# A causal mask on the matrix engine, and head operands that leave PSUM once

## The chip, the core and the metric

The kernel runs on one core of a Trainium2 chip. The core has five engines with an instruction queue each: TensorE (PE in the profile, its weight loads PEld), VectorE (DVE), ScalarE (ACT), GpSimd (POOL) and SyncE (SP), which here only issues DMAs. POOL issues DMAs too. An engine works through its own queue in order and waits at an instruction until all that it needs has been done elsewhere. Matmuls write to PSUM, from which DVE and ACT read; POOL works on SBUF only. The metric is the device time of one execution in microseconds (us); lower is better.

## The reference

Two operators stand one behind the other. The first is attention with chunk selection, on q, k and v of 4 batches, 8 heads, 768 positions and 64 dimensions:

```python
k_chunks = k.reshape(B, H, nc, chunk, D)            # 24 chunks of 32 keys
k_min, k_max = k_chunks.min(3), k_chunks.max(3)
ub = sum(maximum(q * k_min, q * k_max), over D)     # a bound for each query and chunk
ub = where(query's chunk >= chunk, ub, -1e9)
sel = the 6 chunks with the largest ub
scores = where(sel & (query >= key), q @ k.T / 8, -1e9)
out = softmax(scores) @ v
```

Its output, 3072 tokens of 512, is the input of a mixture of experts: a dense two-layer network with relu for every token, and one of eight experts of the same form, picked by a gate, whose result is scaled by the gate's probability and added.

## The kernel before

**Tiling.** Heads are worked in pairs: a pair p (16 of them, four to a batch) has two heads g = 0 and 1 with 64 dimensions each, which together fill 128 partitions. Its 768 positions are six tiles of 128.

**Operands of the scores.** Scores are computed transposed, keys on the partitions, by one matmul for each key tile over the query tiles from there on. Its two operands for head g are `kT[p % 3][g]` and `rT[p % 3][g]`, each 128 partitions x 768 columns of f16, three sets in turn. Head 0 has its keys in rows 0 to 63 of `kT`, and in rows 64 to 95 a constant `exf`, which says with 30000 which chunk a key is in. Head 1 has the constant in rows 0 to 31 and its keys in rows 64 to 127. Opposite them `rT` holds the negated queries and, in the rows of the constant, flags: 1 where a chunk is *not* among the query's six. A score of an unselected key so has 30000 added, and since the exponential is taken with a scale of -0.125 (L555), it becomes zero.

**Preparing a pair** takes six steps, which are written out ahead of the pair's own scores:

- `cast_qk`, `cast_v` (L464 to L476): POOL turns q, k and v from f32 to f16.
- `prep_k` (L478): PE transposes the keys into a PSUM tile `pk`, ACT copies them in order of position to an SBUF tile `kp`, DVE reduces that to the largest and smallest of each chunk (`ks`, L495) and masks these by head (`kb`, L498).
- `prep_q` (L505): PE transposes the queries into `pq`; ACT takes relu of it into `qp` (L513), DVE negates it into the first head's operand, all 128 partitions (L514), and the second head's half into the second's (L515).
- `prep_kt` (L500): DVE copies the halves of `kp` into the two `kT` (L502, L503).
- `prep_ub` (L517): PE computes the bounds from `qp`, the negated queries and `kb`, on top of a causal bias; DVE finds the sixth largest of each row with `max` (L531) and sets the flags (L533).
- `prep_s` (L535): PE transposes the flags and DVE copies them into the flag rows of both `rT` (L541, L542), over the negated queries that the bounds have read.

**The loop over a pair** has eleven units (L210 to L219), each of up to four blocks of 128 keys x 128 queries. In the program's order, unit i of all pairs computes the scores two units ahead, then does one step of preparation (`prep_s` of the next pair at unit 2, `prep_k` of the pair but one at unit 4, `prep_q` at 5, `prep_kt` at 7, `prep_ub` at 9), then fills from the dense network of the batch before, then the product with v (`av`) and the norm of the unit before. Three units of a pair hold the blocks on the diagonal, four each (units 0, 5 and 6). Their exponentials go through POOL, which sets to zero what lies above the diagonal (`affine_select`, L557) before the product with v reads them.

**Order on POOL and SP.** The casts are held behind the last instruction in `latest["pool"]`, which is L557 before the change: `cast_v` of the pair but one at unit 0, `cast_qk` of the third pair ahead at unit 7. Behind them POOL issues weight DMAs (from pair 1 on) and, in batches 1 to 3, scatters the tokens of the batch before to a table in DRAM (L370). SP issues the loads of q, k and v, two buffers each, once a cast has freed one, and stores the dense results.

**PSUM.** In attention three buffers are shared by `pk`, `pq`, `ub`, `ps` and all tiles of the fills, three hold scores and two the products with v.

Behind attention comes the expert stage, with the last batch's dense work beside the expert blocks; its lines (L672 on) are not touched.

Of the kernel before, what the change touches and what calls it, by code (L numbers as in the profile page):

```python
# [10 lines left out]
HF = mybir.dt.float16  # L11
AF = mybir.ActivationFunctionType
ALU = mybir.AluOpType
# [4 lines left out]
def kernel(  # L18
# [12 lines left out]
    nc = tc.nc  # L31
    B, H, S, D = q.shape
# [32 lines left out]
    NJ = 2  # L65
# [10 lines left out]
    acst = att.enter_context(tc.tile_pool(name="acst", bufs=1))  # L76
# [24 lines left out]
    NB = 3  # L101
# [29 lines left out]
                                fill=-60000.0, base=j, pattern=[[128, NT], [0, 2], [-32, NC]], channel_multiplier=2)  # L131
    for i in range(NB):
        nc.vector.memset(kT[i][0][64:128], 0.0)
        nc.vector.memset(kT[i][1][0:64], 0.0)
        nc.vector.memset(v16[i][:, :, :, D : D + 1], 1.0)

    def members():
# [2 lines left out]
        nc.gpsimd.affine_select(out=exf[0:32], in_=exf[0:32], compare_op=ALU.is_ge, fill=0.0,  # L140
                                base=31, pattern=[[-1, S]], channel_multiplier=32)

    def expand(i):
        nc.scalar.copy(kT[i][0][64:96, :], exf[0:32])
        nc.scalar.copy(kT[i][1][0:32, :], exf[0:32])


    iom8 = const.tile([128, NT, E], FP)
# [308 lines left out]
    with (  # L457
# [20 lines left out]
        def prep_k(p):  # L478
            s = st[p]
            pk = pprep.tile([128, S], HF, name="pk", tag="pp")  # L480
            for t in range(NT):
                nc.tensor.transpose(pk[:, t * 128 : (t + 1) * 128], s["k16"][:, t].rearrange("p g d -> p (g d)"), ident)  # L482
            s["kp"] = kp = ahead.tile([128, S], HF, name="kp")
            nc.scalar.copy(kp.rearrange("d (T p j) -> d T p j", p=128, j=NJ),  # L484
                           pk.rearrange("d (T j p) -> d T p j", p=128, j=NJ))
            ks = ahead.tile([128, 2, NC], HF, name="ks")
            if p == 0:

                pc = pk.rearrange("d (T j c w) -> d T c j w", j=NJ, c=8, w=16)
                for i, op in enumerate((ALU.max, ALU.min)):  # L490
                    nc.vector.tensor_reduce(out=ks[:, i].rearrange("d (T c) -> d T c", c=8), in_=pc, op=op,
                                            axis=mybir.AxisListType.XY)
            else:
                for i, op in enumerate((ALU.max, ALU.min)):
                    nc.vector.tensor_reduce(out=ks[:, i], in_=kp.rearrange("d (c w) -> d c w", w=32), op=op,  # L495
                                            axis=mybir.AxisListType.X)
            s["kb"] = kb = ahead.tile([128, 2, 2, NC], HF, name="kb")
            nc.vector.tensor_tensor(kb, ks.unsqueeze(2).to_broadcast([128, 2, 2, NC]), hmask, ALU.mult)  # L498

        def prep_kt(p):  # L500
            kp = st[p]["kp"]
            nc.vector.tensor_copy(kT[p % NB][0][0:64], kp[0:64])  # L502
            nc.vector.tensor_copy(kT[p % NB][1][64:128], kp[64:128])  # L503

        def prep_q(p):  # L505
            s = st[p]
            pq = pprep.tile([128, S], HF, name="pq", tag="pp")
            pqv = pq.rearrange("d (T h j p) -> d T h j p", h=2, j=NJ, p=64)
            for t in range(NT):
                nc.tensor.transpose(pqv[:, t // NJ, :, t % NJ], s["q16"][:, t].rearrange("p g d -> p (g d)"), ident)  # L510
            s["qp"] = qp = ahead.tile([128, S], HF, name="qp")
            r0, r1 = rT[p % NB]
            nc.scalar.activation(qp, pq, AF.Relu)  # L513
            nc.vector.tensor_single_scalar(r0, pq, -1.0, ALU.mult)  # L514
            nc.vector.tensor_single_scalar(r1[64:128], pq[64:128], -1.0, ALU.mult)  # L515

        def prep_ub(p):  # L517

# [2 lines left out]
            nc.tensor.matmul(ub.rearrange("p t g c -> p (t g c)"), ident, cbias.rearrange("p t g c -> p (t g c)"),  # L521
                             start=True, stop=False, skip_group_check=True)
            for t in range(NT):
                for n, (src, j) in enumerate(((s["qp"], 0), (s["qp"], 1), (rT[p % NB][0], 1))):
                    nc.tensor.matmul(ub[:, t].rearrange("p g c -> p (g c)"), src[:, t * 128 : (t + 1) * 128],
                                     s["kb"][:, j].rearrange("p g c -> p (g c)"),
                                     start=False, stop=(n == 2), skip_group_check=True)
# [16 lines left out]
        def scores(p, u):  # L544
            s = st[p]
            pc = units[u]
            sp = psc.tile([128, 512], FP, name="sp")
            o = 0
            for g, kt, a, z in pc:
                w = (z - a) * 128  # L550
                nc.tensor.matmul(sp[:, o : o + w], kT[p % NB][g][:, kt * 128 : (kt + 1) * 128],  # L551
                                 rT[p % NB][g][:, a * 128 : z * 128], start=(o == 0), stop=True, skip_group_check=True)
                o += w
            ex = aexp.tile([128, 512], HF, name="ex")
            nc.scalar.activation(ex[:, 0:o], sp[:, 0:o], AF.Exp, scale=-0.125)  # L555
            if pc[0][1] == pc[0][2]:
                latest["pool"] = nc.gpsimd.affine_select(out=ex, in_=ex, compare_op=ALU.is_ge, fill=0.0, base=0,  # L557
                                        pattern=[[0, 4], [1, 2], [2, 64]], channel_multiplier=-1)
            s["ex", u] = ex

        def av(p, u):
# [260 lines left out]
```

## Time and profile before

| | before |
|---|---|
| median of 3 runs | 255.95 us (254.11 to 255.99) |
| profiled execution | 257.31 us, span 255.5 us |
| busy PE, DVE, ACT, POOL | 84%, 70%, 69%, 62% of the span |
| attention | from about 14 us to 165 us |
| expert stage | from about 165 us to the end |

The span runs from the first to the last instruction of the profiled execution, whose own time is somewhat longer. A group of the profile has the line, the engine, the operation, output and inputs, the count, the busy time in us and the mean duration of one in ns; behind the second bar stands the engine's idle time just before, and what ended it. A wait has its total in us, its count and its longest. A line of the timeline has its start and duration in us. A busy engine is not an engine at its peak: matmuls overlap, and each record lasts until its result is there.

### The profile page before, as it was taken

The numbers are of one execution on the slowest core, as the hardware profiler recorded it, in microseconds if no ns is written. First come the engines' busy times: TensorE is split into PE (matmuls) and PEld (weight loads), VectorE is DVE, ScalarE is ACT, GpSimd is POOL, SyncE is SP. The second block draws the span as 40 slices with busy tenths as digits, with TensorE's granted clock in tenths as the row PEclk, the third lists the DMA queues.
The fourth block names the chain that finished last, engine by engine and source line by source line (L and its number), as shares of the span: only waits on it lengthen the run. The fifth ranks groups of instructions, "written<-read, shape, count | busy, mean of one in ns | idle before, by whom it ended". The sixth has DMA issues, their size and how long they took to land.

```text
span 255.5 us, 7236 instructions
## 1 busy us (share of the span) xinstructions
PE 213.7 (84%) x2547; PEld 141.8 (55%) x2547; DVE 179.3 (70%) x558; ACT 176.1 (69%) x332; POOL 159.6 (62%) x198
## 2 busy tenths in 40 slices
PE   0378969888989899999988988889769999999970
PEld 0256746656657576766567755555335554555530
DVE  6869989999979689998898895167223345555540
ACT  2799979878779898878889778815356555455440
POOL 4746998566276987168986145514744463887881
PEclk9999999999999999999999999999999999999997
DMA  6999999999999799989999924447879999787885
GB/s 172 262 267 228 217 227 239 220 232 202 239 174 292 132 276 226 250 179 242 298 230 258 190 72 128 144 114 218 234 154 208 220 209 200 124 140 97 117 112 105
DMA packets 75124, 50.12 MB, mean 196 GB/s; under 512 B 29648, under 2 KB 68176, under 8 KB 75088
## 3 DMA queue, kind: packets, MB, share of 16 engines
q1 hardware_dynamic: 59856, 30.33, 46.9%
q0 software_dynamic: 15232, 19.32, 45.6%
q8 instruction: 21, 0.34, 0.6%
q14 instruction: 15, 0.12, 0.1%
HBM read 41.93 MB, written 18.23 MB: 235 GB/s over the span
## 4 chain that ended last, share of the span: by engine, by line
PE 29%; DVE 22%; POOL 18%; issue 10%; DMA 7%; ACT 6%; SPq 3%; another core or an unknown queue 1%; POOLq 0%; DVEq 0%; ACTq 0%
DVE ks L495 7%; POOL out_dram L733 7%; PE hp L696 6%; PE yp L725 6%; PE hp L385 4%; POOL ex L557 3%; PE yp L394 3%; POOL table L370 2%; SPq L92 2%; DMA vf<-in_v_dram 2%; ACT ex L555 2%; ACT kp L484 2%; DVE kT L503 2%; DMA kf<-in_k_dram 2%; PE sp L551 2%
## 5 line engine op out<-in xcount | busy, mean ns | idle before, releaser
L555 ACT ACTIVATE ex<-sp 128x512 f16<-128x512 f32 (+1 forms) x176 | 90.9, 608 | 8.9 <-PE sp L551 4.6
L551 PE MATMUL sp<-rT,kT 128*128 128x128 f16 (+3 forms) x384 | 64.4, 260 | 4.0 <-ACT ex L555 2.7
L733 POOL DMA_INDIRECT out_dram<-yo,xg x28 | 43.3, 1545 | 23.5 <-DVE yo L732 9.8
L557 POOL TENSOR_SCALAR_AFFINE_SELECT ex<-ex 128x512 f16<-128x512 f16 x48 | 32.6, 694 | 36.9 <-ACT ex L555 30.8
L570 PE MATMUL op<-v,ex 128*128 128x65 f16 x672 | 48.4, 194 | 3.3 <-POOL ex L557 1.8
L570 PEld LDWEIGHTS <-ex 128*128 128x128 f16 x672 | 36.9, 98 | 19.0 <-POOL ex L557 6.4
L370 POOL DMA_INDIRECT table<-xbig,slot x24 | 23.9, 997 | 20.2 <-issue 15.1
L732 DVE TENSOR_SCALAR yo<-yp,xg 128x512 f32<-128x512 f32 x27 | 20.3, 751 | 22.2 <-PE yp L725 13.3
L551 PEld LDWEIGHTS <-kT 128*128 128x128 f16 x384 | 29.0, 98 | 7.7 <-issue 4.2
L725 PE MATMUL yp<-we,ehT 128*128 x112 | 28.7, 379 | 3.9 <-ACT ys L397 2.5
L707 ACT COPY ehT<-tp 128x512 f16<-128x512 f16 x28 | 16.4, 585 | 21.5 <-PE tp L705 16.7
L696 PE MATMUL hp<-we,exT 128*128 x112 | 29.1, 379 | 2.0 <-DMA xg<-table 1.2
L495 DVE TENSOR_REDUCE ks<-kp 128x24 f16<-128x768 f16 x30 | 27.3, 943 | 4.2 <-ACT kp L484 3.9
L385 PE MATMUL hp<-xT,wd 128*128 128x384 f16 x128 | 26.2, 325 | 0.8 <-DVE xT L258 0.8
L699 ACT ACTIVATE eh<-hp 128x512 f16<-128x512 f32 x28 | 16.7, 597 | 11.4 <-PE hp L696 10.1
L394 PE MATMUL yp<-wd,hT 128*128 128x512 f16 x96 | 23.9, 379 | 0.3 <-issue 0.3
L690 DVE COPY exT<-tp 128x512 f16<-128x512 f16 x28 | 11.8, 423 | 17.4 <-PE tp L688 9.9
L387 ACT ACTIVATE hT<-hp 128x384 f16<-128x384 f32 x32 | 16.1, 505 | 9.0 <-PE hp L385 6.2
L397 ACT COPY ys<-yp 128x512 f32<-128x512 f32 x24 | 14.3, 598 | 9.5 <-PE yp L394 4.3
L484 ACT COPY kp<-pk 128x768 f16<-128x768 f16 x16 | 12.9, 806 | 8.8 <-PE pk L482 8.8
L581 DVE TENSOR_TENSOR xbig<-op,rs 128x384 f16<-128x384 f32 x32 | 17.5, 547 | 0.2
L725 PEld LDWEIGHTS <-ehT 128*128 128x128 f16 x112 | 10.1, 98 | 12.6 <-issue 2.8
(127 smaller groups left out, 383.1 us busy)
## 6 DMA issues: line engine op xcount, KB each, us to landing
we<-in_moe_w_dram POOLq DMA_DIRECT2D x16, 512.0 KB
kf<-in_k_dram SPq DMA_DIRECT2D x32, 192.0 KB
qf<-in_q_dram SPq DMA_DIRECT2D x32, 192.0 KB
vf<-in_v_dram SPq DMA_DIRECT2D x32, 192.0 KB
out_dram<-ys SPq DMA_DIRECT2D x48, 128.0 KB
xg<-table SPq DMA_DIRECT2D x28, 136.0 KB
table<-zt SPq DMA_DIRECT2D x9, 136.0 KB
wd<-in_moe_w_dense_dram POOLq DMA_DIRECT2D x2, 512.0 KB
```

What stands on the lines that cost most here:

```text
L370: sc = nc.gpsimd.indirect_dma_start(out=table, out_offset=bass.IndirectOffsetOnAxis(ap=keep["slot"][:, t : t + 1], axis=0), in_=xbig[b % 2 ...
L385: nc.tensor.matmul(hp, wd[:, ko, j * 128 : (j + 1) * 128], xT[:, ko, g * G * 128 : (g + 1) * G * 128], start=(ko == 0), stop=(ko == NK - 1))
L394: nc.tensor.matmul(yp, hold["h"][:, j, i * 128 : (i + 1) * 128], wd[:, NK + j], start=(j == 0), stop=(j == NK - 1))
L495: nc.vector.tensor_reduce(out=ks[:, i], in_=kp.rearrange("d (c w) -> d c w", w=32), op=op, axis=mybir.AxisListType.X)
L551: nc.tensor.matmul(sp[:, o : o + w], kT[p % NB][g][:, kt * 128 : (kt + 1) * 128], rT[p % NB][g][:, a * 128 : z * 128], start=(o == 0), sto ...
L555: nc.scalar.activation(ex[:, 0:o], sp[:, 0:o], AF.Exp, scale=-0.125)
L557: latest["pool"] = nc.gpsimd.affine_select(out=ex, in_=ex, compare_op=ALU.is_ge, fill=0.0, base=0, pattern=[[0, 4], [1, 2], [2, 64]], chan ...
L570: nc.tensor.matmul(s["op", g][:, t * (D + 1) : (t + 1) * (D + 1)], ex[:, o : o + 128], v16[p % NB][:, g, kt, :], start=first, stop=(last_o ...
L696: nc.tensor.matmul(hp, s["xT"][:, ko], wef[:, bass.ds(offs[i] + ko * 512, 512)], start=(ko == 0), stop=(ko == NK - 1))
L725: nc.tensor.matmul(yp, s["hT"][:, j], wef[:, bass.ds(offs[i] + (NK + j) * 512, 512)], start=(j == 0), stop=(j == NK - 1))
L732: nc.vector.tensor_scalar(o, yp, gate, None, ALU.mult)
L733: sc = nc.gpsimd.indirect_dma_start(out=out, out_offset=to, in_=o, in_offset=None, bounds_check=N - 1, oob_is_err=False, compute_op=ALU.by ...
```

## The change

The mask becomes a matmul. A constant `later` (128 x 128, f16) holds 30000 where a query of the diagonal block comes before the key, and zero elsewhere. In a diagonal unit PE first multiplies the identity with `later`, repeated four times, into the whole scores tile, and the scores are added to it. The exponential then gives zero there, and L557 is gone.

ACT copies the keys from PSUM directly into the second head's `kT`, all 128 partitions, and the reductions read them there; `kp` is gone. For all pairs but the first, POOL then copies rows 0 to 63 to the first head's `kT` and writes the constant over rows 0 to 31 of the second's. Rows 32 to 63 there keep keys of the first head, opposite zeros of the flags.

DVE negates the queries from PSUM once, into the second head's `rT`. For all pairs but the first it then takes relu from that SBUF tile (times -1, then the maximum with 0) in place of ACT's relu from PSUM, and POOL copies rows 0 to 63 to the first head's `rT`. The bounds read the second head's operand in place of the first's. `latest["pool"]` is set by the two last POOL copies of a pair.

The first pair keeps ACT and DVE for these copies.

```diff
@@ constants
-        nc.vector.memset(kT[i][1][0:64], 0.0)
...
+    later = acst.tile([128, 128], HF)
+    nc.vector.memset(later, 0.0)
+    nc.gpsimd.affine_select(out=later, in_=later, compare_op=ALU.is_ge, fill=30000.0, base=0,
+                            pattern=[[1, NJ], [NJ, 64]], channel_multiplier=-1)
     def expand(i):
         nc.scalar.copy(kT[i][0][64:96, :], exf[0:32])
-        nc.scalar.copy(kT[i][1][0:32, :], exf[0:32])
@@ prep_k
-            s["kp"] = kp = ahead.tile([128, S], HF, name="kp")
+            kp = kT[p % NB][1]
             nc.scalar.copy(kp.rearrange("d (T p j) -> d T p j", p=128, j=NJ),
                            pk.rearrange("d (T j p) -> d T p j", p=128, j=NJ))
@@ prep_kt
-            kp = st[p]["kp"]
-            nc.vector.tensor_copy(kT[p % NB][0][0:64], kp[0:64])
-            nc.vector.tensor_copy(kT[p % NB][1][64:128], kp[64:128])
+            k0, k1 = kT[p % NB]
+            if p:
+                nc.gpsimd.tensor_copy(k0[0:64], k1[0:64])
+                latest["pool"] = nc.gpsimd.tensor_copy(k1[0:32], exf[0:32])
+            else:
+                nc.vector.tensor_copy(k0[0:64], k1[0:64])
+                nc.scalar.copy(k1[0:32], exf[0:32])
@@ prep_q
-            nc.scalar.activation(qp, pq, AF.Relu)
-            nc.vector.tensor_single_scalar(r0, pq, -1.0, ALU.mult)
-            nc.vector.tensor_single_scalar(r1[64:128], pq[64:128], -1.0, ALU.mult)
+            if p:
+                nc.vector.tensor_single_scalar(r1, pq, -1.0, ALU.mult)
+                nc.vector.tensor_scalar(qp, r1, -1.0, 0.0, ALU.mult, ALU.max)
+                latest["pool"] = nc.gpsimd.tensor_copy(r0[0:64], r1[0:64])
+            else:
+                nc.scalar.activation(qp, pq, AF.Relu)
+                nc.vector.tensor_single_scalar(r1, pq, -1.0, ALU.mult)
+                nc.vector.tensor_single_scalar(r0[0:64], pq[0:64], -1.0, ALU.mult)
@@ prep_ub
-                for n, (src, j) in enumerate(((s["qp"], 0), (s["qp"], 1), (rT[p % NB][0], 1))):
+                for n, (src, j) in enumerate(((s["qp"], 0), (s["qp"], 1), (rT[p % NB][1], 1))):
@@ scores
+            diag = pc[0][1] == pc[0][2]
+            if diag:
+                nc.tensor.matmul(sp.rearrange("p (n k) -> p n k", k=128), ident, later.unsqueeze(1).to_broadcast([128, 4, 128]),
+                                 start=True, stop=False, skip_group_check=True)
             for g, kt, a, z in pc:
...
-                                 rT[p % NB][g][:, a * 128 : z * 128], start=(o == 0), stop=True, skip_group_check=True)
+                                 rT[p % NB][g][:, a * 128 : z * 128], start=(o == 0 and not diag), stop=True,
+                                 skip_group_check=True)
...
-            if pc[0][1] == pc[0][2]:
-                latest["pool"] = nc.gpsimd.affine_select(out=ex, in_=ex, compare_op=ALU.is_ge, fill=0.0, base=0,
-                                        pattern=[[0, 4], [1, 2], [2, 64]], channel_multiplier=-1)
```

## The prediction

> **What bounds the kernel now.** I read the page first: its busy table, the slices and the shares of the chain that ended last.
>
> ```profile
> span 255.5 us, 7236 instructions
> PE 213.7 (84%) x2547; PEld 141.8 (55%) x2547; DVE 179.3 (70%) x558; ACT 176.1 (69%) x332; POOL 159.6 (62%) x198
> ...
> DVE  6869989999979689998898895167223345555540
> ...
> PE 29%; DVE 22%; POOL 18%; issue 10%; DMA 7%; ACT 6%; SPq 3%; another core or an unknown queue 1%; POOLq 0%; DVEq 0%; ACTq 0%
> ```
>
> No engine bounds the whole span. The DVE digits are 8 or 9 nearly up to slice 23 and fall to half after it: attention, which is all that the change touches, is one stage, the expert blocks another. So next I read busy time by stage: attention without dense work beside it (16 to 48 us), with it (48 to 147), and its last two pairs, which prepare no successor (147 to 165).
>
> ```profile
> 16.00:48.00 32.00, 26.16 (x413) 18.74 (x411) 29.74 (x95) 28.18 (x55) 23.91 (x46) 1.00 1.15 227
> 48.00:147.00 99.00, 90.17 (x1327) 65.94 (x1326) 88.14 (x288) 82.79 (x166) 65.67 (x87) 1.00 1.06 228
> 147.00:165.00 18.00, 16.08 (x197) 10.60 (x195) 10.99 (x50) 15.10 (x32) 9.11 (x12) 1.00 0.39 109
> ```
>
> After the length come PE, PEld, DVE, ACT, POOL. In the first stage DVE is busy 29.74 of 32 us (93%); in the second PE 91%, DVE 89% and ACT 84% stand side by side; in the third DVE has dropped out. Which of them the others wait for is in the table of waits:
>
> ```profile
> POOL ex L557 <- ACT ex L555: 30.8, 19, 6.2
> ...
> PEld L539 <- DVE fl L533: 7.1, 6, 2.4
> ...
> PEld L570 <- POOL ex L557: 6.4, 14, 1.4
> ...
> PEld L510 <- DVE rT L542: 2.4, 2, 1.2
> ```
>
> PE stands in order, and its visible waits in attention are for DVE (flags, copies that free a PSUM buffer) and for the mask on POOL. One turn of the loop in the timeline shows why, from the key transposes of one pair to those of the next:
>
> ```profile
> 38.29 0.50 PE L482 MATMUL pk<-ident,k 128*128 128x128 f16 x6
> ...
> 38.83 0.80 ACT L484 COPY kp<-pk 128x768 f16<-128x768 f16 x1 [1.15 <-PE pk L482]
> ...
> 40.02 1.79 DVE L495 TENSOR_REDUCE ks<-kp 128x24 f16<-128x768 f16 x2
> 41.74 0.54 DVE L514 TENSOR_SCALAR rT<-pq 128x768 f16<-128x768 f16 x1
> 42.21 0.19 DVE L498 TENSOR_TENSOR kb<-ks,hmask 128x96 f16<-128x96 f16 x1
> 42.43 0.56 DVE L515 TENSOR_SCALAR rT<-pq 64x768 f16<-64x768 f16 x1
> 43.01 0.35 DVE L502 COPY kT<-kp 64x768 f16<-64x768 f16 x1
> 43.37 0.76 DVE L503 COPY kT<-kp 64x768 f16<-64x768 f16 x1
> 44.16 0.92 DVE L531 MAX8 m<-ub 128x8 f32<-128x8 f32 x10
> ...
> 45.20 0.46 DVE L533 TENSOR_TENSOR fl<-ub,m 128x288 f16<-128x288 f32 x1
> ...
> 45.71 0.51 PE L539 MATMUL ps<-ident,fl 128*128 128x128 f16 x6 [1.18 <-DVE fl L533]
> ...
> 46.06 0.50 PE L482 MATMUL pk<-ident,k 128*128 128x128 f16 x6
> ```
>
> That is 7.77 us per pair, nearly all DVE back to back from 40.02 to 45.66, at whose end PE has stood 1.18 us. **DVE paces the first stage; DVE and PE together pace the second.** The profiled execution took 257.31 us for a span of 255.5; the median of the runs is 255.95.
>
> **The change part by part.** Means of one instruction, shapes apart:
>
> ```profile
> L557 POOL TENSOR_SCALAR_AFFINE_SELECT ex<-ex 128x512 f16<-128x512 f16 x48 | 32.6, 694 | 36.9 <-ACT ex L555 30.8 <-DMA kf<-in_k_dram 5.4 <-issue 0.4
> ...
> L513 ACT ACTIVATE qp<-pq 128x768 f16<-128x768 f16 x16 | 13.3, 829 | 0.5 <-PE pq L510 0.5
> ...
> L469 POOL CAST k<-kf 128x768 f16<-128x768 f32 x16 | 13.2, 825 | 3.1 <-DMA kf<-in_k_dram 3.1
> ...
> L525 PE MATMUL ub<-kb,qp 128*128 128x48 f16 x192 | 9.6, 185 | 3.2 <-ACT kT L144 2.3 <-DVE kb L498 0.8
> ...
> L515 DVE TENSOR_SCALAR rT<-pq 64x768 f16<-64x768 f16 x16 | 9.0, 561 | 0.5
> ...
> L503 DVE COPY kT<-kp 64x768 f16<-64x768 f16 x16 | 8.0, 500 | 0.3
> ...
> L502 DVE COPY kT<-kp 64x768 f16<-64x768 f16 x16 | 7.0, 437 | 0.1
> ...
> L502 DVE COPY kT<-kp x16: 310/352/794, 11.0 to 150.4; 64x768 f16<-64x768 f16 x16
> ...
> L503 DVE COPY kT<-kp x16: 357/357/860, 11.8 to 150.8; 64x768 f16<-64x768 f16 x16
> ```
>
> *DVE*, for each of 15 pairs: out go L515, L502 and L503, 0.561 + 0.437 + 0.500 = 1.50 us; L514 stays, into the other operand. In comes relu from SBUF. Its nearest rows are the two SBUF copies of the same 768 columns: 0.352 us undisturbed, 0.860 at most; I take 0.47, the mean of their means. Net -1.03 us a pair, -15 us of DVE work, between -1.15 and -0.64 a pair.
>
> The slow copies are a row of their own: the same instruction takes 0.352 or 0.794 us. [...]
>
> *ACT* loses the relu, 15 x 0.829 = 12.4 us, 0.83 of some 8 us a pair, and in the prologue two of six expansion copies. It holds 6% of the chain, so I cost this at nothing by itself: DVE and PE hide it. The query's PSUM buffer has one reader in place of three and comes free earlier.
>
> *POOL* loses 48 selects, 32.6 us busy, and gains three SBUF copies in each of 15 pairs. A 768-column copy between f16 tiles is not in the trace; bounds are 0.55 us (a memset of 544 columns on POOL, below) and 0.825 (the cast above, of the same columns from f32); I take 0.82. 45 x 0.82 = 36.9 us, so POOL's load rises by 4 us and its order changes: the matmuls with values no longer wait for it (6.4 us above), while the casts of the next pair but two now stand behind three copies that wait for DVE.
>
> ```profile
> 35.55 0.55 POOL L185 MEMSET zt<- 128x544 uint16 x1
> ...
> 38.40 0.82 POOL L469 CAST k<-kf 128x768 f16<-128x768 f32 x1
> ```
>
> The key cast began at 38.40, 0.1 us after the transposes at 38.29. In the new order it waits until r1 is written (42.28 in that turn), then for three copies, 2.46: 44.74, ending at 45.6, against transposes due at 46.06. Behind it stand the query cast, the value cast, the weight DMAs POOL issues and the table's scatters, and on SP's queue the next loads of keys and queries with the result stores behind them. The loads have two pairs' time to land. So nothing waits as long as a pair takes over 7.3 us; the first stage can hardly get faster than that.
>
> *A new wait on DVE*: the flags copy into r1's first half must wait for POOL's copy out of it. That copy is due some 3 us earlier in the turn; only norms and the next reductions would queue behind it. At nothing, unless POOL is over 3 us late.
>
> *PE* gains 48 matmuls of 512 columns:
>
> ```profile
> 126.28 1.02 PE L394 MATMUL yp<-wd,hT 128*128 128x512 f16 x4
> ...
> 128.71 0.38 PE L551 MATMUL sp<-rT,kT 128*128 128x512 f16 x1
> ...
> 129.05 0.38 PE L551 MATMUL sp<-rT,kT 128*128 128x512 f16 x1
> ...
> L385 PE MATMUL hp<-xT,wd 128*128 128x384 f16 x128 | 26.2, 325 | 0.8 <-DVE xT L258 0.8
> ...
> L370 POOL DMA_INDIRECT table<-xbig,slot x24 | 23.9, 997 | 20.2 <-issue 15.1
> ...
> L394 PE MATMUL yp<-wd,hT 128*128 128x512 f16 x96 | 23.9, 379 | 0.3 <-issue 0.3
> ```
>
> Four such in 1.02 us, the last alone 0.379 (its mean): 0.215 us each, pipelined. That is 48 x 0.215 = 10.3 us, 0.65 a pair; the identity's weight load overlaps as others do.
>
> Now the **sum by stage**. Prologue: one DVE copy fewer ahead of the first flags, L503 undisturbed, -0.36; I take -0.3.
>
> First stage, four pairs: between kb (42.40) and the maxima (44.16) DVE did 1.76 us of work that goes. In its place stand relu, 0.47, and then what that work covered, the bound matmuls on PE (9.6/16 = 0.60) with a step to each side, 0.1: 1.17. So -0.6 in this turn, and -0.2 where the copies were undisturbed; with the floor at 7.3, -0.3 a pair: **-1.2**.
>
> Second stage, ten pairs: PE's work with the masks is 90.17 + 31 x 0.215 = 96.8 us busy if no wait shrinks; but a busy PE is partly one that streams nothing (the group above holds 0.86 us of streaming in 1.02). From the two scores 0.34 us apart (one unit with its value matmuls), eleven units stream 3.7 us a pair; three sets of transposes 1.05 (ps to pk in the turn above, 0.35 each); bounds 0.7; dense work, per batch of four pairs, 32 matmuls of 384 columns at 0.16 and 24 of 512 at 0.215, 10.3, so 2.6 a pair, and 0.4 of its transposes: 8.45 of 9.9 us, and 9.1 with masks. DVE falls from 8.8 to 7.8. PE is the bound then, at 10.2 pairs x 9.1 = 92.8 at best; PE reached 0.91 of its time by its busy row, so I take a pair at 9.4, 95.8: **-3.2**. Bounds: -6.2, and +6.7 when every mask adds and no wait goes.
>
> Third stage: six masks, 1.3 us, PE busy 16.08 of 18, ACT 15.10, no relief on DVE: I take half, **+0.6**, between 0 and 1.3. The expert stage is not touched: it shifts.
>
> -0.3 - 1.2 - 3.2 + 0.6 = -4.1 us: a span of 251.4, 253.2 by the profiled execution, and 251.9 from the median; I forecast **251.8**.
>
> **The rivals.** *PE takes the masks in full* (slower): in attention with dense work PE, 91% busy, is already the pace, its 8.8 idle us remain where they are, and each mask adds 0.215. That is +6.7 in the second stage and +1.3 in the third, less 1.5: +6.5, **262**. It decides where streaming passes the pair's 9.9 us; I counted 9.1. For it: PE is the largest share of the chain. Against: its listed waits are for DVE and POOL.
>
> *All reliefs add up* (faster still): DVE's 1.03 us a pair shows over ten pairs as 7 us, PE's gaps take the masks, the first stage gains 2: **247**. For it: ACT, DVE and the PSUM buffers are eased at once. Against: PE then streams 9.1 of each 9.2 us.
>
> [...]
>
> **How the numbers follow.** A measurement here tells about 1% (2.6 us) from no change. Forecast (249 to 253.4) 0.45, all reliefs 0.15, POOL in the way 0.20, PE in full 0.20. Faster 0.60, same 0.20, slower 0.20. Leaving out 0.1 at each end, the range is 245.5 to 261: it cuts only the far half of the largest gain and of PE in full, which would be 261 with an eighth of the masks hidden.
>
> **What would show it.** Right: DVE's busy time in attention down by some 14 us, ACT's by 12, PE's up by up to 10, POOL's about level; no wait of value matmuls for POOL; relu near 0.47 us; the turn 0.3 us shorter without dense work and 0.3 with it. PE's share of the chain up, DVE's down. [...]

## The result, and the profile after

The changed kernel takes 282.94 us (280.82 to 285.12, 4 runs), the kernel before 255.97 beside it (254.11 to 256.33, 4 runs): a ratio of **1.104**, 95% interval 1.095 to 1.114. It is 27 us slower, where 4 us faster was forecast. Here and below a time is the median of all executions, while a ratio compares the faster executions of both kernels, since in many of them some executions take 1 to 2% longer. The profiled execution took 283.71 us, its span 282.0. The page of the changed kernel, with the lines that answer to those of before (span, busy time, the DVE slices, and the clock that TensorE was granted):

```profile
span 282.0 us, 7297 instructions
...
PE 233.3 (83%) x2595; PEld 156.1 (55%) x2595; DVE 187.7 (67%) x525; ACT 167.3 (59%) x315; POOL 162.7 (58%) x196
...
DVE  4679697787959597878767897942673335545540
...
PEclk9999598687869799979799988999999999999996
```

DVE has 33 instructions fewer and is busy 8 us *longer*. PE has 48 matmuls more and is busy 20 us longer, at a clock that falls to 0.5 and 0.6 in slices where it stood at 1.0 before. The stages, in the columns of the prediction:

```profile
16.00:48.00 32.00, 25.10 (x332) 18.71 (x331) 26.20 (x66) 20.32 (x40) 19.01 (x39) 0.84 0.98 190
48.00:147.00 99.00, 81.45 (x1033) 58.48 (x1031) 77.23 (x211) 60.13 (x119) 54.03 (x70) 0.86 0.79 173
```

All five engines are less busy than before in the same stretches (PE 81 against 90 of 99 us, ACT 60 against 83). So no engine became the bound; they wait. For what, the table of waits of the changed kernel says:

```profile
PEld L538 <- issue: 15.0, 10, 2.9
PE ub L538 <- DVE kb L501: 14.5, 8, 2.8
...
PE hp L388 <- DVE xT L261: 9.5, 3, 3.5
```

The first two, the matmul and its weight load at the same place, are PE standing in front of the bounds (L538) until DVE has written `kb`, the masked chunk bounds, eight times for up to 2.8 us. Before, that wait was 0.8 us in all, beside 2.3 us that the first pair's bounds waited for a copy on ACT and that are counted under `kb` here. The third line, dense matmuls that wait for a copy on DVE, comes up again below. L501 is the old L498, 128 x 96 elements; nothing in the diff touches it. Its durations (smallest, median, largest in ns), first in the kernel before, then after:

```profile
L498 DVE TENSOR_TENSOR kb<-ks,hmask x16: 193/251/741, 9.7 to 149.0; 128x96 f16<-128x96 f16 x16
```

```profile
L501 DVE TENSOR_TENSOR kb<-ks,hmask x16: 196/3038/3716, 10.5 to 179.3; 128x96 f16<-128x96 f16 x16
```

An instruction of 0.2 us has a median of 3.04. One such place in the timeline of the changed kernel:

```profile
48.79 0.35 DVE L523 TENSOR_SCALAR qp<-rT 128x768 f16<-128x768 f16 x1
...
49.00 0.82 POOL L508 COPY kT<-exf 32x768 f16<-32x768 f16 x1 [0.20 <-DVE ks L498]
...
49.06 3.13 DVE L501 TENSOR_TENSOR kb<-ks,hmask 128x96 f16<-128x96 f16 x1
...
49.77 0.82 POOL L472 CAST k<-kf 128x768 f16<-128x768 f32 x1
50.55 0.82 POOL L474 CAST q<-qf 128x768 f16<-128x768 f32 x1
...
51.32 0.82 POOL L479 CAST v<-vf 128x768 f16<-128x768 f32 x1
52.09 0.75 POOL L209 DMA_DIRECT2D we<-in_moe_w_dram  x1
...
52.25 0.24 PE L538 MATMUL ub<-kb,qp 128*128 128x48 f16 x2 [2.79 <-DVE kb L501]
...
53.10 0.62 PE L568 MATMUL sp<-rT,kT 128*128 128x512 f16 x1
```

`kb` starts 0.06 us after a POOL copy and ends at 52.19, 0.05 us after the last of four POOL instructions that stand back to back (52.14). Each takes 0.82 us and the next starts 0.77 after it: there is no gap between them. It is the same in all nine turns in which `kb` took over 2.9 us: POOL's L508 starts 0.04 to 0.26 us ahead, it opens a row of four or five long SBUF instructions, and `kb` ends with the row. Where POOL issued only scatters beside it (at 101.38, 110.42 and 147.13 us), it took 0.20 to 0.27.

PE waits behind every one of the nine: four times at the bounds for `kb` (2.56 to 2.79 us), twice at the bounds for the relu, which then stands behind `kb` on DVE (3.41 and 2.58), and three times in the dense matmuls (L388) for a copy that DVE does behind `kb` (2.99 to 3.52). That is 26.3 us of waiting. One of each of the two other kinds:

```profile
29.18 0.26 PE L538 MATMUL ub<-kb,qp 128*128 128x48 f16 x2 [3.41 <-DVE qp L523]
...
76.70 1.44 PE L388 MATMUL hp<-xT,wd 128*128 128x384 f16 x4 [3.52 <-DVE xT L261]
```

The step from one pair's key transposes to the next's, in us, read from PE's timeline (first pair to last: 5.84 to 144.87 us before, 6.65 to 175.31 after):

| step | 1 | 2 | 3 | 4 | 5 | 6 | 7 | 8 | 9 | 10 | 11 | 12 | 13 | 14 | 15 |
|---|---|---|---|---|---|---|---|---|---|---|---|---|---|---|---|
| before | 8.4 | 8.0 | 7.1 | 8.9 | 7.8 | 9.0 | 10.4 | 9.1 | 9.2 | 10.4 | 10.9 | 9.0 | 9.8 | 9.7 | 11.3 |
| after | 7.1 | 7.7 | 12.7 | 11.2 | 11.7 | 11.7 | 16.4 | 12.6 | 8.7 | 8.5 | 14.1 | 14.5 | 8.6 | 8.9 | 14.3 |
| `kb` over 2.9 us | | | 3.7 | 3.1 | 3.1 | 3.1 | 3.7 | 3.3 | | | 3.1 | 2.9 | | | 3.1 |

Summed before rounding, the nine steps in which `kb` was held took 119.1 us against 83.6 before, +35.5; the six others 49.6 against 55.5, -5.9. Together +29.6: that is the loss. (After the last key transposes the changed kernel is 4 us shorter, 106.7 against 110.6 us.) The hold itself is 29.3 - 9 x 0.2 = 27.5 us on DVE, and PE's waits behind it are 26.3. What came on top is read from one more row of each kernel, the stretch from 48 to 66 us, first before, then after:

```profile
48.00:66.00 18.00, 15.79 (x255) 11.94 (x254) 17.17 (x55) 13.46 (x28) 10.57 (x15) 1.00 1.09 228
```

```profile
48.00:66.00 18.00, 12.52 (x163) 9.62 (x161) 15.37 (x40) 9.54 (x19) 10.06 (x14) 0.78 0.64 141
```

The granted clock is 0.78 in place of 1.00. Read by quarters of a microsecond from 4 to 176 us, the changed kernel's clock is 0.50 in nine stretches, 41 us in all, and 1.00 between them. Each begins within 1.7 us of the end of one of PE's nine waits, five of them while PE still waits; six last 3.4 us, three 6.8. The kernel before has no such stretch up to 146 us. In the timeline above, the scores of 512 columns right behind the wait take 0.62 us, against 0.38 in the kernel before. The waits beside these stretches were 2.6 to 3.5 us long; what lowers the clock, and what ends a stretch, no run here shows. By estimate, 41 us at half the clock cost up to 20 us of PE's time if it had work throughout. With the 26.3 us of waits that is more than the 35.5 us, so part of it was covered or set off by what the change gained; how the loss divides between waits and clock isn't separated here.

**Theory:** `kb` is held on DVE for the whole of POOL's row, and PE, in order, stands behind what comes out of DVE late. The expectations call it 'port', which was the author's guess at a cause; no run shows a port. **Rivals:** the masks on PE cost the time ('masks'); POOL's own lateness does (three more copies ahead of the casts; 'late chain'); DVE's long `kb` is a wait for data.

### The profile page after: what moved, and what is told of

The parts are those of the page before. It is cut to its first block, busy times and chain, and to the rows that moved or that the text cites. A ratio compares the mean times of both kernels' runs of the same rounds, so it can differ in the third digit from the quotient of the medians.

```text
span 282.0 us, 7297 instructions
## 1 busy us (share of the span) xinstructions
PE 233.3 (83%) x2595; PEld 156.1 (55%) x2595; DVE 187.7 (67%) x525; ACT 167.3 (59%) x315; POOL 162.7 (58%) x196
## 5 line engine op out<-in xcount | busy, mean ns | idle before, releaser
L568 PE MATMUL sp<-rT,kT 128*128 128x128 f16 (+3 forms) x384 | 69.4, 276 | 0.2 <-DVE rT L554 0.2
L585 PE MATMUL op<-v,ex 128*128 128x65 f16 x672 | 54.1, 203 | 0.4 <-ACT ex L573 0.4
L585 PEld LDWEIGHTS <-ex 128*128 128x128 f16 x672 | 42.7, 105 | 16.3 <-issue 5.8
L507 POOL COPY kT<-kT 64x768 f16<-64x768 f16 x15 | 12.3, 823 | 46.8 <-ACT kT L487 46.8
L388 PE MATMUL hp<-xT,wd 128*128 128x384 f16 x128 | 28.9, 350 | 9.5 <-DVE xT L261 9.5
L501 DVE TENSOR_TENSOR kb<-ks,hmask 128x96 f16<-128x96 f16 x16 | 32.7, 2042 | 0.0
L722 ACT COPY ehT<-tp 128x512 f16<-128x512 f16 x28 | 16.4, 586 | 20.3 <-PE tp L720 20.3
L538 PE MATMUL ub<-kb,qp 128*128 128x48 f16 x192 | 11.3, 197 | 20.5 <-DVE kb L501 14.5
L498 DVE TENSOR_REDUCE ks<-kT 128x24 f16<-128x768 f16 x30 | 27.0, 942 | 0.3
L564 PE MATMUL sp<-later,ident 128*128 128x512 f16 x48 | 19.5, 406 | 6.1 <-POOL later L144 5.9
L538 PEld LDWEIGHTS <-qp 128*128 128x128 f16 x192 | 10.8, 105 | 23.5 <-issue 15.0
L400 ACT COPY ys<-yp 128x512 f32<-128x512 f32 x24 | 14.1, 588 | 15.4 <-PE yp L397 15.3
```

Source lines behind the costliest of these rows:

```text
L388: nc.tensor.matmul(hp, wd[:, ko, j * 128 : (j + 1) * 128], xT[:, ko, g * G * 128 : (g + 1) * G * 128], start=(ko == 0), stop=(ko == NK - 1))
L585: nc.tensor.matmul(s["op", g][:, t * (D + 1) : (t + 1) * (D + 1)], ex[:, o : o + 128], v16[p % NB][:, g, kt, :], start=first, stop=(last_o ...
```

## The experiments

Each ratio is to the kernel before on the same chip (254.6, 256.47, 255.29 and 258.75 us there; the chips differ).

**The mask alone** (`mask_only`): the kernel before with the masks multiplied in, no other part. The casts, which were ordered behind L557, are ordered behind one another.

```diff
+            if diag:
+                nc.tensor.matmul(sp..., ident, later..., start=True, stop=False, ...)
-            if pc[0][1] == pc[0][2]:
-                latest["pool"] = nc.gpsimd.affine_select(out=ex, ...)
```

> The kernel before with the mask by matmul alone; the casts on POOL are held behind the cast before them. Theory 'port': no POOL copies, so kb stays under 0.5 us; 253 to 261 us with the clock above 0.98. Theory 'masks': most of the 27 us is here, 272 us or more, and the clock falls below 0.95. The prediction's price for all masks on PE's path was +8 us (264).

Measured: 256.94 us, ratio 1.007 (1.003 to 1.011), at a granted clock of 0.984 to 0.995. The masks cost 1.8 us net of the selects that POOL no longer does, not 27, and not the 8.0 at which the rival that PE takes them in full had priced them (6.7 and 1.3).

**The change without the mask** (`no_mask`): the matmuls out, L557 back.

```diff
-            if diag:
-                nc.tensor.matmul(sp..., ident, later..., start=True, stop=False, ...)
+                latest["pool"] = nc.gpsimd.affine_select(out=ex, ...)
```

> The changed kernel with the mask back on POOL: copies on POOL, relu on DVE and single reading of PSUM stay. Theory 'port': kb still means over 1.5 us and the time is 272 us or more, since POOL has 33 us more to do. Theory 'masks': 252 to 260 us, clock 0.98 or more.

Measured: 281.12 us, ratio 1.103 (1.088 to 1.118). So the loss stays without the mask. It isn't the same loss throughout: `kb` has a mean of 1.06 us here (over 1.5 was expected), relu 0.66, and the products' weight loads wait 20.0 us for selects that now stand behind copies.

**`kb` away from DVE** (`kb_act`): four small ACT instructions with a column of 0 and 1, or 0 and -1, as scale.

```diff
-            nc.vector.tensor_tensor(kb, ks.unsqueeze(2).to_broadcast([128, 2, 2, NC]), hmask, ALU.mult)
+            for i in range(2):
+                for g in range(2):
+                    nc.scalar.activation(kb[:, i, g], ks[:, i], AF.Copy, scale=hcol[:, 2 * i + g : 2 * i + g + 1])
```

> The changed kernel, with kb computed by four small ACT instructions (each chunk extreme times a column per partition) in place of DVE's product of two SBUF tiles. [...] Theory 'masks' (48 more matmuls fill PE and lower its clock): 275 us or more, clock still under 0.95. [...]

Measured: 277.82 us, ratio 1.081 (1.068 to 1.094). By its time alone this run would speak for the masks, which the two runs above rule out; now the relu is held, in the same way. Its timeline and, behind it, its waits:

```profile
51.20 0.82 POOL L515 COPY kT<-exf 32x768 f16<-32x768 f16 x1 [1.18 <-DVE ks L503]
...
51.56 3.75 DVE L530 TENSOR_SCALAR qp<-rT 128x768 f16<-128x768 f16 x1
...
54.28 0.82 POOL L484 CAST v<-vf 128x768 f16<-128x768 f32 x1
```

```profile
PEld L545 <- DVE qp L530: 21.0, 7, 4.6
```

The relu ends at 55.31, the row at 55.10. So it is no property of `kb`: relu, with a single SBUF input, is held as well. Six of its 15 took 2.98 to 4.78 us.

**Relu back on ACT** (`relu_act`), `kb` left on DVE:

```diff
-                nc.vector.tensor_scalar(qp, r1, -1.0, 0.0, ALU.mult, ALU.max)
+                nc.scalar.activation(qp, pq, AF.Relu)
```

> The changed kernel with relu alone back on ACT; kb stays on DVE. Theory 'port': kb now starts at the end of the reductions, when POOL still waits for the same end to overwrite the keys, so it mostly comes first: mean under 1.2 us and 250 to 265 us; where it loses, it again takes about 3 us. Theory 'late chain': 270 us or more.

Measured: 276.31 us, ratio 1.066 (1.055 to 1.076). The expectation was missed in size: a relu fewer on DVE moves `kb` to another place beside the row, and it is held over 2 us in six pairs (up to 3.84) rather than in nine.

**Both away from DVE** (`free_port`): `kb` on POOL, relu on ACT.

```diff
-            nc.vector.tensor_tensor(kb, ks..., hmask, ALU.mult)
+            nc.gpsimd.tensor_tensor(kb, ks..., hmask, ALU.mult)
-                nc.vector.tensor_scalar(qp, r1, -1.0, 0.0, ALU.mult, ALU.max)
+                nc.scalar.activation(qp, pq, AF.Relu)
```

> [...] All POOL copies and the masks on PE stay. [...]

Measured: 272.39 us, ratio 1.048 (1.042 to 1.054), not the 247 to 255 us that the author expected. The second to the last key transposes lie 128.5 us apart, against 130.7 before, so the hold is gone; but the first `kb` stood on POOL behind casts that wait for their loads (PE waits 7.8 us for it), and some 11 us went at the end of attention.

**The same, first pair's `kb` on DVE** (`free_port2`):

```diff
+            (nc.gpsimd if p else nc.vector).tensor_tensor(kb, ks..., hmask, ALU.mult)
```

> As the run with kb on POOL and relu on ACT, but the first pair's kb stays on DVE (there kb stood 5 us behind casts that waited for their DMA). Theory 'port': 5 us less than that run, 265 to 269 us by its chip, with the middle of attention as before; the rest of its loss was between the last key transposes and the last exponential (31 us against 20 before), where DVE waited 3.7 us for POOL's value cast.

Measured: 258.12 us from two runs only (255.71 and 260.54), without an interval; span 254.0. That is less than the 265 to 269 us expected: beside the 5 us of the first `kb`, the loss at the end of attention didn't come back either, and why isn't known. Of one kernel with two runs no more is concluded than that most of the 27 us can go once neither `kb` nor relu stands on DVE beside the row.

**The copies back on DVE and ACT** (`copies_dve`), with the mask by matmul and the single reading of PSUM; the casts are ordered behind one another:

```diff
-                nc.gpsimd.tensor_copy(k0[0:64], k1[0:64])
-                latest["pool"] = nc.gpsimd.tensor_copy(k1[0:32], exf[0:32])
+                nc.vector.tensor_copy(k0[0:64], k1[0:64])
+                nc.scalar.copy(k1[0:32], exf[0:32])
-                latest["pool"] = nc.gpsimd.tensor_copy(r0[0:64], r1[0:64])
+                nc.vector.tensor_copy(r0[0:64], r1[0:64])
```

> The changed kernel with the three POOL copies a pair back on DVE (queries and keys) and ACT (the constant); mask by matmul, single reading of PSUM and relu from SBUF on DVE stay. Theory 'port': no row of POOL instructions beside kb and relu, both under 0.6 us in the mean; 251 to 258 us. By the prediction's rows DVE is 0.4 us a pair lighter than before the change and ACT about level. Theory 'late chain': 251 to 258 as well; this run sizes the rest of the change.

Measured: 263.62 us, ratio 1.014 (1.007 to 1.021), over the 251 to 258 us expected, on the chip on which the kernel before took 258.75. Taking POOL's copies away takes most of the loss away, not all: what is left of the change gains nothing here.

**One reading of PSUM alone** (`one_read`): as the run before, with the mask on POOL and relu on ACT, so that what is left of the change is DVE's relief (and a constant that ACT writes for each pair).

```diff
-            if diag:
-                nc.tensor.matmul(sp..., ident, later..., start=True, stop=False, ...)
+                latest["pool"] = nc.gpsimd.affine_select(out=ex, ...)
-                nc.vector.tensor_scalar(qp, r1, -1.0, 0.0, ALU.mult, ALU.max)
+                nc.scalar.activation(qp, pq, AF.Relu)
```

> The part of the change that relieves DVE, alone: keys and negated queries leave PSUM once, the halves are copied from SBUF on DVE, the constant by ACT for each pair; the mask stays on POOL, relu on ACT. By the rows of before DVE loses 0.56 + 0.44 + 0.50 and gains two copies of 0.35, 0.8 us a pair; ACT gains 0.83 for the constant. The prediction's view that DVE paces attention: 250 to 254 us. If PE's order paces it and DVE's work is covered: 255 to 259 us.

Measured: 258.10 us, ratio 1.009 (1.003 to 1.014). The second stage of this kernel:

```profile
48.00:147.00 99.00, 88.37 (x1302) 64.24 (x1300) 83.18 (x276) 88.24 (x174) 66.48 (x88) 1.00 1.04 220
```

DVE is busy 83.18 of 99 us, 5 less than before, and the kernel is no faster: ACT has risen from 82.79 to 88.24, with the constant that it writes for each pair. DVE didn't pace this stage alone; how much it would have gained with ACT left as it was, this run can't say.

**The order alone** (`gate`): the changed kernel, same copies on POOL, but two copies of one element (0.18 us each), which read `kb` and `qp`, stand ahead of them. POOL's row so starts after DVE is done with both.

```diff
+                nc.gpsimd.tensor_copy(tick[0:1, 0:1], s["kb"][0:1, 0, 0, 0:1])
+                gate = nc.gpsimd.tensor_copy(tick[0:1, 1:2], qp[0:1, 0:1])
+                with tc.issue_after(gate.ins):
+                    latest["pool"] = nc.gpsimd.tensor_copy(r0[0:64], r1[0:64])
...
+                with tc.issue_after(latest["pool"].ins):
+                    nc.gpsimd.tensor_copy(k0[0:64], k1[0:64])
+                    latest["pool"] = nc.gpsimd.tensor_copy(k1[0:32], exf[0:32])
```

> The changed kernel, with each instruction where it was, but for two POOL copies of one element a pair, from kb and from relu's result, ahead of POOL's three copies, which are held behind them. So DVE does kb and relu before the row of copies and casts begins. Theory 'port': kb and relu fall to under 0.6 us each in the mean, PE's waits for them to under 5 us, and the time to 253 to 262 us. Theory 'late chain' (it is the lateness of POOL's copies and casts that costs): the copies are later still, so 280 us or more.

Measured: 256.11 us, ratio 0.993 (0.987 to 0.999), and on another chip, with more runs:

> The ordered kernel once more (the changed kernel, POOL's copies held until kb and the relu are done; bundled with two one-element copies on POOL), to set it beside the next one on one chip. Theory (port): 253 to 257 us beside a kernel before of 256, ratio 0.985 to 1.0; kb below 0.25 us on average, relu at 0.35. If the first measurement was a matter of its chip: ratio over 1.02.

Measured: 255.91 us, ratio 0.997 (0.991 to 1.002). No work was taken away, two instructions a pair were added, and 27 us are gone. The place of the timeline above, and the durations of `kb`, in the first of the two:

```profile
49.06 0.35 DVE L526 TENSOR_SCALAR qp<-rT 128x768 f16<-128x768 f16 x1
...
49.33 0.20 DVE L503 TENSOR_TENSOR kb<-ks,hmask 128x96 f16<-128x96 f16 x1
...
49.48 0.18 POOL L528 COPY tick<-qp 1x1 f16<-1x1 f16 x1 [1.73 <-DVE qp L526]
...
49.60 0.82 POOL L530 COPY rT<-rT 64x768 f16<-64x768 f16 x1
```

```profile
L503 DVE TENSOR_TENSOR kb<-ks,hmask x16: 190/201/751, 10.5 to 151.2; 128x96 f16<-128x96 f16 x16
```

This is the run that decides between the theory and its rivals. A wait for data would be there still (`kb` needs the same reductions), the masks are there, and POOL's copies and casts come *later* behind the key transposes than in the changed kernel. From 48 to 66 us the clock is 1.00 again and PE busy 17.68 of 18 us: the low clock went with the waits. What the runs show is that `kb` takes 2.9 to 3.7 us where it starts just behind the first copy of POOL's row, and 0.20 where it goes ahead of the row; by what POOL holds DVE isn't seen in a trace. What this run leaves open to gain stands in its waits:

```profile
POOL tick L528 <- DVE qp L526: 17.5, 7, 5.2
...
POOL tick L527 <- DVE kb L503: 10.5, 4, 4.4
PEld L487 <- POOL k L474: 10.4, 7, 5.1
```

Of the 10.4 us in the last line, 5.1 are the first pair's, which the changed kernel has as well (5.8 before). The other six waits, 5.3 us, are new: the casts stand behind the copies that wait, and key transposes wait for the casts.

**A shorter row** (`casts_first`): the changed kernel, the casts of k and q one step of the loop earlier, ahead of the key preparation.

```diff
+            if u == 3:
+                with tc.issue_after(latest["pool"].ins):
+                    cast_qk(p + 3)
+                load(p + 5, "kq")
             if u == 4 and n2 is not None:
                 prep_k(n2)
...
-                with tc.issue_after(latest["pool"].ins):
-                    cast_qk(p + 3)
-                load(p + 5, "kq")
```

> The changed kernel with the key and query casts one step of the loop ahead of the key preparation instead of behind POOL's copies, so that the row that POOL does without a pause is two instructions shorter. Theory 'port', held through the whole row: kb falls from 2.04 us in the mean to between 0.8 and 1.5, and the time to 262 to 275 us. [...]

Measured: 267.49 us, ratio 1.046 (1.035 to 1.057); the mean of `kb` falls from 2.04 to 1.50 us, its median from 3.04 to 1.30. Where the row was L508 and the value cast alone (at 37.76, 46.20 and 54.83 us), `kb` took 1.59 to 1.81. A shorter row so made a shorter hold here. In two turns (at 25.80 and 64.20 us, 3.59 and 3.75 long) it went on beside the weight DMAs that POOL issued behind the casts, which it didn't do in the changed kernel; the second of them ended with the key cast behind the DMA.

That a hold lasts to the end of the row is not a rule, though. At 80.21 us of this kernel `kb` was done after 1.00 us, 0.16 us into the value cast that stood back to back with the copies. In the kernel before, `kb` started at 127.60 us beside the key cast (127.16 to 128.00) and was done at 128.08, although the query cast had begun at 127.93. What decides whether DVE gets in between two POOL instructions isn't shown.

**Both** (`gate_casts`): the order and the early casts. To `gate` it adds

```diff
+            if u == 3:
+                with tc.issue_after(latest["pool"].ins):
+                    cast_qk(p + 3)
+                load(p + 5, "kq")
...
-                with tc.issue_after(latest["pool"].ins):
-                    cast_qk(p + 3)
-                load(p + 5, "kq")
```

> The ordered kernel with the casts of q and k for the third pair ahead one step of the loop earlier, ahead of the key preparation. In the ordered kernel PE's weight loads waited 10.4 us for POOL's cast of the keys, because the casts now stand behind copies that wait for kb and relu. Theory (what is left is POOL's order): those waits go, kb stays below 0.3 us, ratio 0.96 to 0.99 to the kernel before, 247 to 254 us. Rival (the casts, issued earlier, lie beside the reductions, relu or kb of another pair and hold them): kb or relu above 0.6 us on average, ratio 1.0 to 1.05. Second rival (PE is the bound by now): the waits go elsewhere and the ratio stays at 0.985 to 1.0.

Measured: 253.67 us, ratio **0.982** (0.976 to 0.987): by the ratio 4.7 us faster than the kernel before, and faster than `gate` on the same chip (0.997). Its page:

```profile
span 250.1 us, 7308 instructions
...
PE 219.6 (88%) x2595; PEld 147.2 (59%) x2595; DVE 164.1 (66%) x525; ACT 166.0 (66%) x315; POOL 168.4 (67%) x226
```

The waits of weight loads for the key cast are gone but for the first pair's 5.1 us. The other rival is there in part: the early casts hold `kb` again in four turns (three of 0.82 us, one of 1.71), and its mean is 0.44 us where under 0.3 was expected. This is the version that beats both kernels.

**The ordered kernel with the mask on POOL** (`gate_select`): the matmuls out of `gate`, the selects back.

```diff
-            if diag:
-                nc.tensor.matmul(sp..., ident, later..., start=True, stop=False, ...)
+                nc.gpsimd.affine_select(out=ex, ...)
```

> The ordered kernel with the mask back on POOL (48 selects of 0.69 us, no mask matmuls). It prices the mask beside POOL copies that do not hold DVE. Theory: PE is freed of 48 matmuls of about 0.41 us, but POOL, with three copies and three selects a pair, comes late with selects that stand behind waiting copies, and the product with v waits: ratio 1.03 to 1.10. Rival (the mask on PE is what keeps the ordered kernel from gaining): ratio 0.95 to 0.985.

Measured: 267.76 us, ratio 1.053 (1.047 to 1.060), 5.7% over `gate`. Its waits:

```profile
PEld L589 <- POOL ex L576: 22.6, 30, 3.5
...
PE op L589 <- POOL ex L576: 14.9, 17, 3.2
```

The products with v wait for selects again, far more than in the kernel before (6.4 us at the weight loads). With three copies a pair on POOL, the mask is better on PE here.

**Idle copies in the kernel before** (`before_copies`, `mask_copies`): three POOL copies a pair into a tile that nobody reads, in the places of the change's copies, with the casts held behind them; in the second with the mask by matmul.

```diff
+                nc.gpsimd.tensor_copy(idle[0:64, 0], kp[0:64])
+                latest["pool"] = nc.gpsimd.tensor_copy(idle[0:32, 1], exf[0:32])
...
+                latest["pool"] = nc.gpsimd.tensor_copy(idle[64:128, 0], r1[64:128])
```

> The kernel before plus three POOL copies a pair into a scratch tile that nobody reads (from r1, kp and the chunk constant, where the change has its copies), with the casts held behind them as in the change. Nothing else moves. Theory 'port': kb rises from 0.36 us to over 1.2 in the mean and the time to 264 us or more, though no result depends on these copies. Theory 'masks': 254 to 260 us, kb under 0.6.

> The kernel with the mask by matmul alone (256.9 us measured) plus three POOL copies a pair into a scratch tile that nobody reads, with the casts behind them; no product with v waits for POOL here, unlike in the first run with such copies, where the selects stood behind them and kb rose to 0.61 us only. [...] Theory 'late chain' (results that wait for copies): nothing waits for them, 255 to 260 us.

Measured: 280.12 us, ratio 1.099 (1.090 to 1.109), and 281.81 us, ratio 1.087 (1.080 to 1.094). The times look like the theory's, but `kb` doesn't: means of 0.61 us, where over 1.2 was expected, and 0.43. In the second `kb` and the two key copies come to 1.56 us a pair, where the author expected over 3. `kb` also got in between two POOL instructions that stood back to back (at 89.09 us of the first, 0.82 us long, and at 30.53 us of the second, 0.56). In the first, products with v wait for selects behind the copies (22.1 us, up to 6.8 at once). In the second, POOL's copies themselves wait, for table transfers (17.6 us) and for DVE, and the casts with them. So in these two the loss is of another kind, and they don't bear the theory out. To see what the second one's loss was, its copies were held until DVE was done with `kb` and the keys (`mask_copies_gate`):

```diff
+                nc.gpsimd.tensor_copy(tick[0:1, 0:1], st[p]["kb"][0:1, 0, 0, 0:1])
+                gate = nc.gpsimd.tensor_copy(tick[64:65, 1:2], kT[p % NB][1][64:65, 0:1])
+                with tc.issue_after(gate.ins):
+                    nc.gpsimd.tensor_copy(idle[0:64, 0], kp[0:64])
+                    nc.gpsimd.tensor_copy(idle[0:32, 1], exf[0:32])
+                    latest["pool"] = nc.gpsimd.tensor_copy(idle[64:128, 0], rT[p % NB][1][64:128])
```

> The kernel before with the mask matmul and three idle POOL copies per pair, as the run that came out at 1.087, but the copies held until kb and DVE's copy of the second head's keys are done. The copies and casts so come later on POOL than in that run, but lie less beside DVE's instructions with two SBUF inputs or with SBUF alone. Theory (in that run too the row of copies beside DVE cost the time): DVE's kb at 0.2 and the key copies at 0.35 and 0.76 us, ratio 1.0 to 1.03. Rival (there the loss was POOL's lateness: casts and table transfers behind three more copies): ratio 1.06 to 1.12 and weight loads of the key transposes waiting for POOL's casts.

Measured: 298.51 us, ratio 1.170 (1.163 to 1.178), with DVE's copies and `kb` undisturbed (means 0.37, 0.44 and 0.26 us). Its waits:

```profile
PEld L490 <- POOL k L477: 44.8, 11, 10.2
PE pk L490 <- POOL k L477: 42.8, 9, 10.0
```

The rival holds here, beyond the 1.06 to 1.12 expected of it: a POOL that comes late with its casts costs as much as the hold does. The four longest of these waits, 6.2 to 10.2 us, come right behind four in which POOL's own one-element copy stood for the table transfers, 32.8 us in all; so most of the lateness was theirs. In the changed kernel it isn't the cause (the wait of weight loads for the key cast is 5.1 us, once), but it shows how little room POOL has.

## Why the prediction was wrong

**The step that failed** is the one on DVE. It counted three instructions out and the relu in, and left the rest of DVE's work at its durations of before. A longer duration was weighed for the relu alone (0.47 us, between 0.352 and 0.860); `kb` was not looked at. In the trace `kb` is held beside POOL's copies and casts (2.9 to 3.7 us), and not beside its scatters (0.20 to 0.27).

**"POOL in the way"**, at 0.20 the case of no change, named the resource and was priced too low. A row was there to see in the prediction's own words, "Behind it stand the query cast, the value cast": three or four of 0.82 us each behind the copy. Measured is 27.5 us of hold, 3.05 us on average in nine pairs, and the steps of these pairs are 3.9 us longer. The prediction also watched the wrong instruction. The relu came out at 0.352 us in the median, 0.397 in the mean (0.47 was taken), since it mostly starts in the 0.2 us in which POOL waits for the reductions, just ahead of L508, or when the row has ended. None of the signs that the prediction lists names `kb`; pairs of over 10 us came, with PE 82% busy in the second stage.

**PE in order** makes the hold dear. The prediction kept `kb` to bounds at a step of 0.1 us. The nine waits come to 26.3 us: behind them on PE stand scores, products and fills, and then comes the half clock, 41 us of it.

The other steps, in turn:

- *Prologue*, -0.3: right; the first scores start at 15.07 us against 15.49.
- *POOL's copy*, 0.82 us: right. Groups of the changed kernel:

```profile
L524 POOL COPY rT<-rT 64x768 f16<-64x768 f16 x15 | 12.5, 833 | 7.8 <-DVE rT L522 7.8
...
L508 POOL COPY kT<-exf 32x768 f16<-32x768 f16 x15 | 12.3, 822 | 6.3 <-DVE ks L498 6.2
```

- *The flag copies' new wait*, at nothing: right; no such wait is in the table.
- *POOL's order*, "nothing waits as long as a pair takes over 7.3 us": half right. Without the hold, the first four steps do come to 7.1 to 7.8 us in `gate` and `gate_casts`, at that floor; but beyond the first pair 5.3 us of weight loads wait for casts in `gate`, and with the casts earlier the ratio goes from 0.997 to 0.982.
- *The masks*, 0.65 us a pair: too much. Alone they cost 1.8 us net of the selects, and PE's busy time in `gate_casts` is 5.9 us above before, not 10.3. *PE takes the masks in full* fell by that; that it had the sign of the result is luck.
- *"DVE paces the first stage"*: not borne out as a source of gain; `one_read`, with 5 us less on DVE in the second stage and 2 in the first, gained nothing, with ACT 5.5 us fuller.
- *The second stage's sum* is inconsistent in itself: it takes 10.2 pairs at 9.4 us, but its 99 us hold ten pairs at 9.9. With ten the term would be -5, not -3.2; neither the sign nor the failed step depends on it.

Once the hold is taken out and the casts come early, the steps of the first four pairs sum to 29.8 us (before 32.5) and the next ten to 91.1 (95.3). That is -2.6 and -4.2, where -1.2 and -3.2 were forecast: the sum's size was that of a kernel in which DVE's two instructions go first. Whether it comes about by the sum's own mechanism isn't shown; `one_read` rather speaks against DVE's part.

**Open:** by what POOL's row holds DVE; what lowers the granted clock; how the loss divides between PE's waits and the half clock behind them; what decides whether DVE gets in between two POOL instructions of a row; and why `free_port` lost 11 us at the end of attention and `free_port2` didn't.

## What to carry to other kernels

When work is moved to GpSimd, list the DVE instructions that can fall beside it, the ones that the change doesn't touch too, and price each at up to what is left of GpSimd's *whole row*, not at one instruction (here up to 3.7 us for a `kb` of 0.2). Then look who stands in order behind the held instruction. Where the two become ready at the same moment, let the short DVE instruction go first, by a one-element read on GpSimd if need be: here the same work took 27 us less that way. Against that, whatever stands behind on GpSimd's queue gets later, so what others wait for is to be issued ahead of the copies.

## What the runs showed of the hardware that was not expected

- A DVE instruction of 0.2 us was held for four or five GpSimd instructions in a row, 2.9 to 3.7 us, up to 4.78 for the relu in `kb_act`. GpSimd's instructions of 0.82 us follow at 0.77 us, and in none of the nine turns did it get in between two of them. In other kernels here it did (at 127.60 us of the kernel before it took 0.48 us beside two casts).
- A lead of 0.05 us can make the price: in the turn shown, the relu started 0.2 us ahead of POOL's copy and took 0.35 us, `kb` started 0.06 behind it and took 3.13.
- A GpSimd copy of 768 f16 columns takes as long for 32 partitions as for 64 (0.822 and 0.823 to 0.833 us), and as long as its cast from f32 (0.820).
- Each of nine waits of PE, 2.56 to 3.52 us long, went with a granted clock of 0.50 for 3.4 us (six times) or 6.8 us (three times); in `gate` the clock was 1.00 from 48 to 66 us, where the changed kernel had 0.78. In `casts_first` holds of 1.6 to 1.8 us brought no such stretch.
